# Scores of windowed attention in a different bank layout, v in five slots, and a new instruction list

## The chip, the core and the metric

One NeuronCore of a Trainium2 chip runs the whole program. Time is device time in microseconds (us) of one execution. TensorE (PE in the rows) multiplies; VectorE (DVE), ScalarE (ACT) and GpSimd (POOL) do the elementwise work; SyncE (SP) issues every DMA. Results of TensorE lie in 8 PSUM banks of 128 x 512 fp32.

## What is computed

Two parts, one feeding the other, all in fp32 from the outside:

```python
scores = scale * q @ k.T                     # 8 batches, 8 heads, 576 positions, head_dim 64
rel = pos[:, None] - pos[None, :]
mask = (rel >= 0) & (rel < 128)              # a causal window of 128
scores = where(mask, scores - slope[h] * |rel|, -1e9)
attn = softmax(scores);  x = attn @ v        # heads side by side: x is 576 x 512 per batch
h = gelu_tanh(x @ w_in);  u, g = halves of h
g = layernorm(g) * g_ln
out = x + (u * (w_sg @ g + b_sg)) @ w_out
```

With blocks of 64 positions, a query sees its own key block up to the diagonal, the block before it whole, and of the block before that only the keys that the own block's mask leaves out. So own block and third block share one 64 x 64 square: each place of it belongs to one of the two.

## The kernel before, in words

Heads are taken two at a time: 8 batches x 4 give 32 **pairs**, numbered n = 0 to 31. The gated MLP of a batch b follows its four pairs. All work is cut into **steps**, each a letter and a number, and a list of about 1,900 names (`ORDER`, L803) gives one order from which every engine takes its own steps, in that order. Nothing is reordered behind it: a step that waits holds everything behind it on its engine. `Planner.run` (L408) only gives out the PSUM banks and checks that a buffer is free by then.

Steps of a pair, with the line that runs them: `q` loads q and k (L218, one DMA of 576 KB), `L` loads v (L225 to L229); `a` and `c`, from pair 5 on together as `*`, are the scores on TensorE (L244); `A B C G` are the minima on VectorE, one for each head and two tiles of 128 queries: a `copy_predicated` (L272) folds the third block into the own block's square, and two `tensor_tensor_reduce` (L263, three where the first 64 queries are) add the bias and keep the row's extreme; `e E f F` are the exponentials on ScalarE (L281), `j` those of the first 64 queries; `R` (L293, L294) makes the inverse sums on VectorE; `s S r` scale on GpSimd (L298); `t T z` transpose on TensorE (L308, L321); `X Y` split a transposed bank by a mask (L316, L317) and write `px`; `P` copies the first queries' part (L324); `V` multiplies by v (L340, L345, L349); `x` gathers (L360, L362), `h l k` split into two fp32r parts.

The MLP's steps (`u v tt y O` on TensorE, L576 to L578, L660 to L662, L724, L725) are fp32r products in three terms. The opening also splits the int64-viewed fp64 weights w_in into two parts: `i` load (L167), `d` (L178, L180) on ScalarE, `b o` on VectorE (L182, L184), `+` on GpSimd (L187), `H` and `-`. `w` are single products of the first batch, used as soon as their quarter of the weights is split. `D` (L777) stores the output.

**Scores.** fp32 products have two matmul records each in the trace. A product here has a 64 x 64 stationary part, so the array holds four at a time: head j uses array rows 64j on, and the query half picks the array columns. Before, query half 0 of both heads goes to PSUM partitions 0 to 63 and half 1 to partitions 64 to 127, and each tile of 128 queries fills 192 columns (three key blocks) for either half.

**v.** `vt` has ten slots of 64 + 64 rows, and seven DMAs fill them, with each block of v present twice.

**The masks.** `sel` (128 x 128 uint8) steers the fold, `m_own` the split, `bias` (128 x 256 for each head, L134, ScalarE) the slopes; they are made before the first step.

Of the kernel before, what the change touches and what calls it, by code (L numbers as in the profile page):

```python
# [9 lines left out]
F32 = mybir.dt.float32  # L10
# [11 lines left out]
def attention_gmlp(  # L22
# [19 lines left out]
    P = 128  # L42
# [18 lines left out]
    psum = [ps.tile([P, 512], F32, name=f"bank{i}") for i in range(NB)]  # L61
    given = []
# [23 lines left out]
    ident = const.tile([P, P], F32, name="ident")  # L86
    make_identity(nc, ident)


# [3 lines left out]
    def twice(x):  # L93
        nc.scalar.copy(x[R:P], x[0:R])

    def temp(name, dt=F32):
        return mlp.tile([P, P], dt, name=name, tag="g", bufs=NF)[0:R, 0:R]

    ones = temp("ones")
    nc.vector.memset(ones, 1.0)  # L100


    m_own = halves("m_own", 4 * R)
    lo = temp("lo")
    nc.gpsimd.affine_select(out=lo, in_=ones, pattern=[[1, R]], compare_op=ALU.is_ge, fill=0.0, base=0, channel_multiplier=-1)
    nc.vector.memset(m_own, 1.0)

    for rs, cs in ((slice(R, P), slice(0, 2 * R)), (slice(0, R), slice(2 * R, 4 * R))):
        nc.scalar.copy(m_own[rs, cs].rearrange("p (h c) -> p h c", h=2), over(lo, 2))

    sel_f = temp("sel_f")
    nc.gpsimd.affine_select(out=sel_f, in_=ones, pattern=[[1, R]], compare_op=ALU.is_gt, fill=0.0, base=0, channel_multiplier=-1)
    sel = halves("sel", 2 * R, U8)
    for rs in (slice(0, R), slice(R, P)):
        nc.scalar.copy(sel[rs, 0:R], sel_f)
        nc.scalar.activation(sel[rs, R:2 * R], sel_f, AF.Copy, scale=-1.0, bias=1.0)


# [4 lines left out]
    rel = mlp.tile([P, NF, S], F32, name="rel", tag="u")[:, 0, 0:4 * R]  # L123
    nc.vector.tensor_copy(rel[0:R, 0:R], rel_i)
    nc.vector.tensor_scalar(rel[0:R, R:2 * R], rel[0:R, 0:R], float(R), None, ALU.add)
    nc.vector.scalar_tensor_tensor(out=rel[0:R, 0:R], in0=sel_f, scalar=float(P), in1=rel[0:R, 0:R], op0=ALU.mult, op1=ALU.add)
    nc.scalar.copy(rel[0:R, 2 * R:4 * R].rearrange("p (b c) -> p b c", b=2), over(rel[0:R, 0:R], 2))
    twice(rel)
    nc.vector.scalar_tensor_tensor(out=rel[0:R, 3 * R:4 * R], in0=sel_f, scalar=1e9 / min(slopes), in1=rel[0:R, 0:R], op0=ALU.mult, op1=ALU.add)

    biases = []
    for h in range(H):
# [4 lines left out]
    p0s = [const.tile([P, R], F32, name=f"p0_{i}") for i in range(3)]  # L137

    e0s = []
    for i in range(2):  # L140
        x = const.tile([P, 2 * R], F32, name=f"e0_{i}")
        nc.gpsimd.memset(x, 0.0)
        e0s.append(x)

    NS = 2 * (T + 1)
    stats = []
    for i in range(3):
        x = const.tile([P, 2, NS + 1], F32, name=f"stats{i}")
        nc.vector.memset(x, 1.0)
        stats.append(x)  # L150


# [52 lines left out]
    class Pair:  # L205


        def __init__(self, n):
            self.n, self.b, self.hp = n, n // NPAIR, n % NPAIR
            self.p0 = p0s[n % 3]  # L210
            self.nm, self.sm = [stats[n % 3][:, i, :] for i in range(2)]
# [694 lines left out]
```

## Time and profile before

| what | value |
|---|---|
| time before | 611.9 us, median of 3 runs: 607.64, 611.9, 612.24 |
| the profiled execution | 608.44 us, its span 606.7 us, mean granted clock 0.987 |
| busy: TensorE, VectorE, ScalarE, GpSimd | 580.5, 377.5, 364.9, 231.4 us |
| HBM read, written | 47.88, 9.44 MB |

The span is from the first to the last instruction; 1.7 us lie around it. The profile page gives busy time by engine and by 40 slices, then groups of instructions by source line. Two matmuls overlap in the pipeline, so TensorE's busy time says when it worked and not how fast; how far one start is behind the next tells that.

### The profile page before, as it was taken

The numbers are of one execution on the slowest core, as the hardware profiler recorded it, in microseconds if no ns is written. First come the engines' busy times: TensorE is split into PE (matmuls) and PEld (weight loads), VectorE is DVE, ScalarE is ACT, GpSimd is POOL, SyncE is SP. The second block draws the span as 40 slices with busy tenths as digits, with TensorE's granted clock in tenths as the row PEclk, the third lists the DMA queues.
The fourth block names the chain that finished last, engine by engine and source line by source line (L and its number), as shares of the span: only waits on it lengthen the run. The fifth ranks groups of instructions, "written<-read, shape, count | busy, mean of one in ns | idle before, by whom it ended". The sixth has DMA issues, their size and how long they took to land.

```text
span 606.7 us, 16591 instructions
## 1 busy us (share of the span) xinstructions
PE 580.5 (96%) x6496; PEld 535.9 (88%) x6496; DVE 377.5 (62%) x1348; ACT 364.9 (60%) x1145; POOL 231.4 (38%) x234
## 2 busy tenths in 40 slices
PE   3679999999999999999999999999999999999997
PEld 3457999899898999999999899998999899998997
DVE  5898988566574775456846675746747367625422
ACT  9789796733755459483776549563384656543420
POOL 3677556530173312713164322524118330461030
PEclk8879999999999999999999999999999999999999
DMA  8997533213062425403150175222243013200102
GB/s 259 254 258 206 134 83 87 86 59 88 37 182 72 95 68 139 119 10 98 46 142 2 59 182 127 85 79 88 68 120 98 7 58 107 86 2 1 40 21 97
DMA packets 56450, 58.39 MB, mean 96 GB/s; under 512 B 4914, under 2 KB 45874, under 8 KB 56372
## 3 DMA queue, kind: packets, MB, share of 16 engines
q1 hardware_dynamic: 56372, 57.34, 34.2%
q8 instruction: 51, 0.84, 0.6%
q14 instruction: 27, 0.22, 0.1%
HBM read 47.88 MB, written 9.44 MB: 94 GB/s over the span
## 4 chain that ended last, share of the span: by engine, by line
PE 88%; DMA 6%; SPq 2%; ACT 1%; POOL 1%; issue 1%; DVE 0%; POOLq 0%
PE bank L576 22%; PE bank L577 21%; PE bank L578 21%; PE bank L244 7%; PE bank L340 5%; PE bank L308 4%; PE bank L345 3%; DMA qk<-qkT 3%; PE bank L725 1%; PE bank L724 1%; DMA vt<-v_in 1%; PE bank L660 1%; PE bank L662 1%; SPq L227 1%; DMA wst<-w_in 1%; POOL g L739 1%
## 5 line engine op out<-in xcount | busy, mean ns | idle before, releaser
L281 ACT ACTIVATE e<-e,stats 128x128 f32<-128x128 f32 (+1 forms) x320 | 121.2, 381 | 31.5 <-DVE stats L263 31.0
L298 POOL TENSOR_TENSOR e<-e,rr 128x512 f32<-128x512 f32 (+1 forms) x96 | 79.8, 850 | 151.6 <-DVE rr L294 139.0
L576 PE MATMUL bank<-ws,vn 128*128 128x288 f32 x256 | 78.3, 306 | 0.0
L576 PE MATMUL bank<-g,wo 128*128 128x288 f32 x256 | 77.7, 304 | 0.0
L576 PE MATMUL bank<-xs,wi 128*128 128x288 f32 x256 | 76.8, 300 | 0.0
L577 PE MATMUL bank<-g,wo 128*128 128x288 f32 x256 | 75.7, 296 | 0.3 <-POOL g L739 0.3
L578 PE MATMUL bank<-g,wo 128*128 128x288 f32 x256 | 75.6, 295 | 0.0
L578 PE MATMUL bank<-xs,wi 128*128 128x288 f32 x256 | 75.6, 295 | 0.0
L577 PE MATMUL bank<-xs,wi 128*128 128x288 f32 x256 | 75.6, 295 | 0.0
L577 PE MATMUL bank<-ws,vn 128*128 128x288 f32 x256 | 75.5, 295 | 0.0
L578 PE MATMUL bank<-ws,vn 128*128 128x288 f32 x256 | 75.4, 295 | 0.0
L601 POOL TENSOR_TENSOR rs<-rs,mhalf 128x1 f32<-128x1 f32 (+1 forms) x40 | 29.7, 746 | 112.3 <-DVE rs L598 112.2
L244 PE MATMUL bank<-qk 64*64 64x192 f32 (+2 forms) x1280 | 56.6, 319 | 12.2 <-DMA qk<-qkT 12.2
L263 DVE CUSTOM_DVE_ANT_0 e<-bank,bias 128x128 f32<-128x128 f32 (+1 forms) x256 | 59.2, 269 | 2.3
L739 POOL TENSOR_TENSOR g<-u,g 128x576 fp32r<-128x576 f32 x32 | 45.3, 1431 | 39.8 <-ACT g L736 32.5
L281 ACT ACTIVATION_READ_ACCUMULATOR e<-e,stats 128x1 f32 (+1 forms) x320 | 60.4, 189 | 0.0
L244 PEld LDWEIGHTS bank<-qk 64*64 64x64 f32 x1280 | 45.5, 141 | 15.8 <-DMA qk<-qkT 13.4
L316 DVE TENSOR_TENSOR px<-bank,m_own 128x512 f32<-128x512 f32 x64 | 43.7, 682 | 22.2 <-PE bank L308 17.8
L370 POOL TENSOR_TENSOR xs<-xf,xs 128x576 fp32r<-128x576 f32 x32 | 45.3, 1422 | 29.0 <-ACT xs L367 29.0
L272 DVE COPY_PREDICATED bank<-sel,bank 128x128 f32<-128x128 uint8 x128 | 36.5, 285 | 28.1 <-PE bank L244 28.1
L576 PE MATMUL bank<-wi,xs 128*128 128x512 f32 x128 | 51.8, 404 | 1.6 <-ACT xs L367 1.6
L578 PE MATMUL bank<-wi,xs 128*128 128x512 f32 x128 | 50.9, 397 | 1.8 <-POOL xs L370 1.8
(109 smaller groups left out, 1451.8 us busy)
## 6 DMA issues: line engine op xcount, KB each, us to landing
qk<-qkT SPq DMA_DIRECT2D x32, 576.0 KB, 4.4
vt<-v_in SPq DMA_DIRECT2D x192, 64.0 KB, 3.5
outT<-xf SPq DMA_DIRECT2D x32, 288.0 KB, 2.4
vt<-v_in SPq DMA_DIRECT2D x32, 256.0 KB, 4.5
wst<-w_in SPq DMA_DIRECT2D x8, 512.0 KB, 6.1
wst<-w_out SPq DMA_DIRECT2D x4, 512.0 KB, 4.5
wst<-w_sgT SPq DMA_DIRECT2D x4, 288.0 KB, 5.5
wst<-w_sgT SPq DMA_DIRECT2D x2, 144.0 KB, 4.7
```

Of the source, the lines that this page charges most:

```text
L244: return lambda: nc.tensor.matmul(dst, qk[js, 0, q0:q0 + R], qk[js, 1, k0:k1], start=True, stop=True)
L263: nc.vector.tensor_tensor_reduce(out=dst, in0=src, in1=bs, scale=-1.0 / math.sqrt(D), scalar=3e38, op0=ALU.add, op1=ALU.min, accum_out=acc)
L272: nc.vector.copy_predicated(bank[:, 2 * R:4 * R].rearrange("p (i c) -> p i c", i=2), sel.rearrange("p (i c) -> p i c", i=2), ends)
L281: nc.scalar.activation(x, x, AF.Exp, bias=self.nm[0:n, i:i + 1], scale=-1.0, accum_out=self.sm[0:n, i:i + 1])
L298: nc.gpsimd.tensor_tensor(x, x, self.rr[0:n, i:i + m].rearrange("p (m o) -> p m o", o=1).broadcast_to([n, m, c]), ALU.mult)
L316: nc.vector.tensor_tensor(xv[:, 0], cv, over(m_own, 2), ALU.mult)
L340: return lambda: nc.tensor.matmul(dst(q)[heads[j]], vt[:, PAIR_SLOT[q], heads[j]], px[j][:, (q - 1) * R:q * R], start=(q in (1, 3)), stop= ...
L370: nc.gpsimd.tensor_tensor(lo_of(self.xs), self.xf, hi_of(self.xs).bitcast(F32), ALU.subtract)
L576: nc.tensor.matmul(dst, ah, bh, start=(first and i == 0), stop=False)
L577: nc.tensor.matmul(dst, ah, bl, start=False, stop=False)
L578: nc.tensor.matmul(dst, al, bh, start=False, stop=(last and i == n - 1))
L739: nc.gpsimd.tensor_tensor(st[f"g{f}"][:, 1, :], st["u"][:, f, :], st[f"g{f}"][:, 0, :].bitcast(F32), ALU.subtract)
```

## The change

- **Scores** (L244 before): each query block's own and previous key block are 128 columns at the front of a 256-column half bank, the third key block lies at columns 128 on of it. Of the two query blocks of a tile, one has its three key blocks in one product of 192 columns, the other one of 128 and one of 64. Head 1 swaps the partition halves against head 0. The first 64 queries take the place of the third block that query block 1 doesn't have. 24 products a pair instead of 20, 1,536 streamed columns a head instead of 1,600.
- **Fold**: `copy_predicated` now works on 128 x 2 x 128 instead of 128 x 2 x 64, with a mask `sel0` or `sel1` for either head. The parts of the banks it may read are cleared once at the start (`clear`, eight memsets on VectorE).
- **First queries**: both heads' in columns 64 to 127 of `e0`, head 0 on rows 0 to 63 and head 1 on rows 64 to 127, so one exponential of 128 x 64 in place of two of 64 x 64; after the transpose they lie on rows 64 to 127.
- **v**: five slots, three DMAs (256, 32 and 32 KB) instead of seven (256 and six of 64 KB).
- **Sums**: the 1e-9 is written once beside each sum, and `tensor_reduce` over the two replaces `tensor_scalar`.
- **Gather**: three copies instead of four. **Split**: a mask for each head, same number of elements.
- **Setup**: biases of heads 2 to 7 on GpSimd, `ident` and the split masks later.
- **Output**: in the last batch, each quarter is stored in two DMAs of 144 KB.
- **A new ORDER**, of which two or three places are shown below.

The diff, cut to its core:

```diff
+    def clear(x):
+        nc.vector.memset(x.rearrange("p (t c) -> p t c", t=2)[:, :, P:2 * P], 0.0)
...
+    def bias(h):
         x = halves(f"bias{h}", 4 * R)
-        nc.scalar.activation(x, rel, AF.Copy, scale=-slopes[h] * math.sqrt(D))
+        of = rel[:, h % 2 * 4 * R:(h % 2 + 1) * 4 * R]
+        if h < 2:
+            nc.scalar.activation(x, of, AF.Copy, scale=-slopes[h] * math.sqrt(D))
+        else:
+            nc.gpsimd.tensor_scalar(x, of, -slopes[h] * math.sqrt(D), None, ALU.mult)
...
-            vt = self.vt = att.tile([P, 2 * T + 2, 2 * D], F32, name="vt", bufs=2)
-            blocks = v[b, :, c0:c0 + 2 * D].rearrange("(k p) d -> p k d", p=R)
-            nc.sync.dma_start(vt[0:R, 0:2 * T, :], blocks[:, 0:2 * T, :])
-            for slot, k in ((0, 1), (1, 2), (2, 0), (3, 2)):
-                nc.sync.dma_start(vt[R:P, slot:slot + 5:4, :], blocks[:, k:k + 5:4, :])
-            for rs, k in ((slice(0, R), 4), (slice(R, P), 3)):
-                nc.sync.dma_start(vt[rs, 2 * T:2 * T + 2, :], blocks[:, k:k + 5:4, :])
+            vt = self.vt = att.tile([P, T + 1, 2 * D], F32, name="vt", bufs=2)
+            src = v[b, :, c0:c0 + 2 * D]
+            nc.sync.dma_start(vt[:, 0:T, :], src[0:T * P].rearrange("(k p) d -> p k d", p=P))
+            nc.sync.dma_start(vt[0:R, T, :], src[T * P:S])
+            nc.sync.dma_start(vt[R:P, T, :], src[0:R])
...
             for i in range(2):
-                for half in range(2):
-                    q0 = R + (t2 + i) * P + half * R
-                    for j, js in enumerate(heads):
-                        dst = banks[j][half * R:(half + 1) * R, i * W:(i + 1) * W]
-                        if q0 < P:
-                            insts += [score(dst[:, 0:R], js, q0, 0, R), score(dst[:, R:W], js, q0, 0, P)]
-                        else:
-                            insts.append(score(dst, js, q0, q0 - P, q0 + R))
-            if t2 == 0:
-                insts += [score(banks[j][0:R, 2 * W:2 * W + R], js, 0, 0, R) for j, js in enumerate(heads)]
+                q, d = 1 + 2 * (t2 + i), 4 * i
+                insts += [score(j, 0, d, q, q - 1, q + 1) for j in range(2)]
+                insts += [score(j, 1, d, q + 1, q - 1, q + 2) for j in range(2)]
+                insts += [score(j, 0, d + 3, q, q - 2, q - 1) if q > 1 else score(j, 0, d + 3, 0, 0, 1) for j in range(2)]
...
-            ends = bank.rearrange("p (k c) -> p k c", c=R)[:, 0:6:5, :]
-            nc.vector.copy_predicated(bank[:, 2 * R:4 * R].rearrange("p (i c) -> p i c", i=2), sel.rearrange("p (i c) -> p i c", i=2), ends)
+            sv = bank.rearrange("p (t c) -> p t c", t=2)
+            nc.vector.copy_predicated(sv[:, :, 0:P], sels[j][:, 0:2] if t2 == 0 else sels[j][:, 1:3], sv[:, :, P:2 * P])
...
         def exps_first(self):
-            for j in range(2):
-                self.exp(self.e0[0:R, j * R:(j + 1) * R], 2 * T + j)
+            self.exp(self.e0[:, R:P], 2 * T)
...
-            nc.vector.tensor_scalar(rr, self.sm, 1e-9, None, ALU.add)
+            nc.vector.tensor_reduce(out=rr, in_=self.sm, axis=mybir.AxisListType.X, op=ALU.add)
...
+            insts = [both(t, s, j) for t in range(T) for s in range(2) for j in range(2)]
+            for t in range(T):
+                insts += [rest(t, 0, j) if t else first(j) for j in range(2)]
+                insts += [rest(t, 1, j) for j in range(2)]
             burst(insts)
...
-            add(f"D{b}{c}", "SP", 0.5, at, lambda: nc.sync.dma_start(out[b, cs, :], x[c]), [f"oa{b}{c}0", f"oa{b}{c}1"], lag=2.5)
+            if b == B - 1:
+                for i in range(2):
+                    add(f"D{b}{c}{i}", "SP", 0.5, at, lambda i=i: nc.sync.dma_start(out[b, cs, halves[i]], x[c][:, halves[i]]), [f"oa{b}{c}{i}"], lag=2.5)
```

Rows of the order show the new list at the places below; each row is a source line (of before or of the change), an operation, what it writes from what it reads, and its size. First, TensorE before: the end of V of pair 5 (L345 and L349, px and p times v) and the start of the scores of pair 6 (L244).

```order
L349 MATMUL bank_67<-p_2_126,vt 64x64
L345 MATMUL bank_70<-px,vt 64x64
L349 MATMUL bank_70<-p_2_126,vt 64x64
L244 MATMUL bank_72<-qk 64x64
L244 MATMUL bank_72<-qk 64x128
L244 MATMUL bank_69<-qk 64x64
L244 MATMUL bank_69<-qk 64x128
L244 MATMUL bank_72<-qk 64x192
L244 MATMUL bank_69<-qk 64x192
```

TensorE of the change, the scores (L254) of a whole pair's burst at their end, and the V (L339) that follows them; the MLP's products stand ahead of such a burst and behind such a V.

```order
L254 MATMUL bank_68<-qk 64x128
L254 MATMUL bank_70<-qk 64x128
L254 MATMUL bank_68<-qk 64x192
L254 MATMUL bank_70<-qk 64x192
L254 MATMUL bank_68<-qk 64x64
L254 MATMUL bank_70<-qk 64x64
L339 MATMUL bank_72<-px,vt 64x64 x2
L339 MATMUL bank_71<-px,vt 64x64 x2
```

The scores of a tile of queries went from one product of 192 columns in each of the four array parts to 128, 192 and 64, and a V now follows a burst where a burst followed a V. From pair 5 to the end a burst directly behind a V occurs 21 times before and 6 times in the change, and a V directly behind a burst 3 times and 20 times.

SP before, the DMAs of the opening up to the loads of pairs 4 and 5 (qk x2): two loads of v with seven DMAs each and two of w_in.

```order
L225 DMA vt<-v_in 64x8x128
L227 DMA vt<-v_in 64x2x128 x4
L229 DMA vt<-v_in 64x2x128 x2
L167 DMA wst<-w_in 128x512
L225 DMA vt<-v_in 64x8x128
L227 DMA vt<-v_in 64x2x128 x4
L229 DMA vt<-v_in 64x2x128 x2
L167 DMA wst<-w_in 128x512
L218 DMA qk<-qkT 128x1152 x2
```

SP of the change, the same stretch.

```order
L238 DMA vt<-v_in 128x4x128
L239 DMA vt<-v_in 64x128
L240 DMA vt<-v_in 64x128
L180 DMA wst<-w_in 128x512
L238 DMA vt<-v_in 128x4x128
L239 DMA vt<-v_in 64x128
L240 DMA vt<-v_in 64x128
L180 DMA wst<-w_in 128x512
L566 DMA gb<-g_ln 128x512
L231 DMA qk<-qkT 128x1152 x2
```

Ahead of pair 4's qk, one w_in load of 512 KB fewer and each of the three v loads half as large; a load of 256 KB (gb) moved ahead of it.

ScalarE before, at the start: after the first two biases come six more, then the first copies of a weight (L178, L180).

```order
L94 COPY rel<-rel 64x256
L134 ACTIVATE bias_108<-rel 128x256
L134 ACTIVATE bias_110<-rel 128x256
```

ScalarE of the change, the same place: head 0's bias (bias_109), which the first minimum needs, stands behind the two copies of a weight (L191, L193) that wait for that weight's DMA.

```order
L119 COPY rel<-rel 64x256
L118 COPY rel<-rel 64x256
L191 ACTIVATE wst<-wst 128x512
L127 ACTIVATE bias_113<-rel 128x256
L193 ACTIVATE tmp<-wst 128x512
L127 ACTIVATE bias_109<-rel 128x256
```

The biases of the first two heads went from ahead of the first weight to between and behind its two copies.

## Rows read from the trace of the kernel before

**Rows 1.** The page: span, and busy time by engine.
```profile
span 606.7 us, 16591 instructions
PE 580.5 (96%) x6496; PEld 535.9 (88%) x6496; DVE 377.5 (62%) x1348; ACT 364.9 (60%) x1145; POOL 231.4 (38%) x234
```
**Rows 2.** Stretches: us, busy by engine with counts, granted clock, DMA share, GB/s.
```profile
30.00:45.00 15.00, 10.36 (x171) 8.08 (x171) 14.26 (x54) 13.31 (x46) 12.27 (x11) 0.77 0.92 259
45.00:60.00 15.00, 13.96 (x169) 10.76 (x166) 12.37 (x49) 14.75 (x58) 11.12 (x10) 1.00 0.71 196
300.00:400.00 100.00, 100.00 (x1213) 93.83 (x1206) 62.80 (x252) 67.05 (x210) 41.13 (x39) 1.00 0.35 91
```
**Rows 3.** TensorE's waits, whole span: us in total, times, longest.
```profile
PE bank L244 <- DMA qk<-qkT: 12.2, 5, 4.7
```
**Rows 4.** TensorE's waits from 60 us on.
```profile
PE bank L244 <- DMA qk<-qkT: 2.0, 2, 1.2
```
**Rows 5.** The ending chain in order of time: start us, us, what.
```profile
35.30 5.68 DMA qk<-qkT
41.03 1.00 PE bank L244 x20
...
143.41 0.64 SPq L227
...
147.35 5.77 DMA qk<-qkT
153.16 3.12 PE bank L244 x64
...
603.10 0.46 DVE xf L762
```
**Rows 6.** The chain where a V follows a burst of scores.
```profile
101.19 1.58 PE bank L244 x34
102.77 1.08 PE bank L340 x32
...
104.57 0.48 PE bank L308 x3
```
**Rows 7.** The chain where a burst of scores follows a V.
```profile
173.95 1.08 PE bank L340 x32
...
175.76 1.48 PE bank L244 x31
177.24 0.58 PE bank L308 x4
```
**Rows 8.** Groups by line and shape: line, engine, shapes, count, busy us, mean ns.
```profile
L244 PE MATMUL bank<-qk 64*64 64x192 f32 x896 | 55.8, 348 | 0.0
L244 PE MATMUL bank<-qk 64*64 64x64 f32 x256 | 21.5, 235 | 12.2 <-DMA qk<-qkT 12.2
L345 PE MATMUL bank<-px,vt 64*64 64x64 f32 x896 | 22.3, 227 | 0.0
L272 DVE COPY_PREDICATED bank<-sel,bank 128x128 f32<-128x128 uint8 x128 | 36.5, 285 | 28.1 <-PE bank L244 28.1
L293 DVE TENSOR_SCALAR rr<-stats 128x11 f32<-128x11 f32 x32 | 9.1, 286 | 26.8 <-ACT e L281 26.8
```
**Rows 9.** VectorE's sum operation: shortest, median, longest ns.
```profile
L293 DVE TENSOR_SCALAR rr<-stats x32: 108/172/1261, 14.4 to 531.0; 128x11 f32<-128x11 f32 x32
```
**Rows 10.** VectorE and ScalarE in order of time: start, us, what.
```profile
6.91 0.29 DVE L263 CUSTOM_DVE_ANT_1 e<-bank,bias 128x128 f32<-128x128 f32 x1
...
7.34 0.66 ACT L178 ACTIVATE wst<-wst 128x512 int32<-128x512 uint32 x1
```
**Rows 11.** The stretch from 8.57 to 51.20 us, columns as in Rows 2.
```profile
8.57:51.20 42.63, 27.88 (x442) 21.43 (x443) 38.00 (x155) 37.42 (x143) 32.05 (x28) 0.84 0.93 257
```
**Rows 12.** Loads of v: count, KB each, median us from issue to landing.
```profile
vt<-v_in SPq DMA_DIRECT2D x192, 64.0 KB, 3.5
vt<-v_in SPq DMA_DIRECT2D x32, 256.0 KB, 4.5
```

More of the change, by code (lines that the diff above doesn't have):

```diff
@@ L85, in attention_gmlp @@
     nc.scalar.activation(warm, mhalf, AF.Exp)
-    ident = const.tile([P, P], F32, name="ident")
-    make_identity(nc, ident)
     def halves(name, n, dt=F32):
         return const.tile([P, n], dt, name=name)
-    def twice(x):
-        nc.scalar.copy(x[R:P], x[0:R])
     def temp(name, dt=F32):
-        return mlp.tile([P, P], dt, name=name, tag="g", bufs=NF)[0:R, 0:R]
+        return const.tile([P, R], dt, name=name)[0:R]
     ones = temp("ones")
     nc.vector.memset(ones, 1.0)
[L103 to L111, printed above, removed]
+    for x in psum[0:4]:
+        clear(x)
+    half = [slice(0, R), slice(R, P)]
+    lo, sel_f = temp("lo"), temp("sel_f")
     nc.gpsimd.affine_select(out=sel_f, in_=ones, pattern=[[1, R]], compare_op=ALU.is_gt, fill=0.0, base=0, channel_multiplier=-1)
[L113 to L116, printed above, removed]
     slopes = [2.0 ** (-8.0 * (h + 1) / H) for h in range(H)]
@@ L131, in attention_gmlp @@
+    nc.vector.scalar_tensor_tensor(out=kinds[0:R, 3], in0=sel_f, scalar=1e9 / min(slopes), in1=own, op0=ALU.mult, op1=ALU.add)
+    nc.vector.tensor_copy(kinds[0:R, 2], kinds[0:R, 0])
+    nc.vector.tensor_copy(kinds[0:R, 4:8:2], over(kinds[0:R, 1], 2))
+    nc.vector.tensor_copy(kinds[0:R, 5:8:2], over(kinds[0:R, 0], 2))
+    nc.scalar.copy(rel[R:P, 0:4 * R], rel[0:R, 4 * R:8 * R])
+    nc.scalar.copy(rel[R:P, 4 * R:8 * R], rel[0:R, 0:4 * R])
     biases = []
-    for h in range(H):
+    def bias(h):
@@ L139, in attention_gmlp @@
+        biases.append(x.rearrange("p (b c) -> p b c", b=4))
+    for x in psum[4:]:
+        clear(x)
+    sels = [halves(f"sel{j}", 3 * P, U8).rearrange("p (t c) -> p t c", t=3) for j in range(2)]
+    for x in sels:
+        nc.gpsimd.memset(x, 0)
+    for j, x in enumerate(sels):
+        bias(j)
+        nc.scalar.copy(x[half[j], 1:3, R:P], over(sel_f, 2))
+        nc.scalar.activation(x[half[1 - j], :, 0:R], over(sel_f, 3), AF.Copy, scale=-1.0, bias=1.0)
     e0s = []
     for i in range(2):
-        x = const.tile([P, 2 * R], F32, name=f"e0_{i}")
+        x = const.tile([P, P], F32, name=f"e0_{i}")
@@ L153, in attention_gmlp @@
+    m_owns = [halves(f"m_own{j}", P) for j in range(2)]
+    for j, x in enumerate(m_owns):
+        nc.gpsimd.memset(x, 1.0)
+    for j, x in enumerate(m_owns):
+        nc.scalar.copy(x[R:P, half[j]], lo)
+        nc.scalar.activation(x[0:R, half[1 - j]], lo, AF.Copy, scale=-1.0, bias=1.0)
+    for h in range(2, H):
+        bias(h)
+    p0s = [const.tile([P, P], F32, name=f"p0_{i}") for i in range(3)]
     wi = const.tile([P, 2, NC, 2 * F], F32R, name="wi")
@@ L351, in values, with dst, src @@
-            insts = [pair(q, j) for a, b in ((1, 3), (2, 4), (5, 7), (6, 8)) for q in (a, b) for j in range(2)]
-            insts += [old(3, 0), old(2, 0), old(3, 1), old(2, 1), old(4, 0), old(5, 0), old(4, 1), old(5, 1)]
-            insts += [old(7, 0), old(6, 0), old(7, 1), old(6, 1), old(8, 0), first(1), old(8, 1), first(0)]
+            def dst(t, s, j):
+                return x1[s][heads[j], t * R:(t + 1) * R]
+            def src(rs, i, t, s, j):
+                c0 = (i * T + t) * P
+                return px[j][rs, c0 + (s ^ j) * R:c0 + (s ^ j) * R + R]
```

219 lines of the change are left out of this document (107 added, 112 removed).

## The prediction

> **What bounds the kernel now.** I read the page first, then TensorE's busy time by stretch, then its waits, then the ending chain. The page gives TensorE 580.5 of 606.7 us [rows 1]. In a stretch of the middle it is busy for all of 100 us at full granted clock, with VectorE at 62.80 and ScalarE at 67.05 [rows 2]. There only the length of TensorE's own list counts. In the opening it is otherwise: from 30 to 45 us TensorE works 10.36 us of 15 at a mean granted clock of 0.77, while VectorE works 14.26, ScalarE 13.31, and the DMA engines are 0.92 busy [rows 2]. Three resources are near their limit there at once. TensorE's waits say the same: 12.2 us for qk in all [rows 3], of which 2.0 us fall from 60 us on [rows 4]. So there are four places to cost: the opening, TensorE's list, the later waits, and the end.
>
> **Burst of scores.** The chain shows a pair's burst as 1.48 us where a V is ahead of it [rows 7] and 1.58 us where the MLP or a transpose is ahead and a V behind it [rows 6]. Is it paid by columns or by products? 64x64 records last 235 ns and 64x192 records 348 ns in the trace [rows 8], so 128 columns more take 113 ns and 64 columns some 55. The busiest array part carries 832 columns before (64, 128, 192, 64 for the first tiles, twice 192 for the rest), 13 units of 64, each streamed by two records: 13 x 2 x 0.055 = 1.43 us, close to the 1.48. So columns on the busiest part set it, and the four parts run side by side. The change puts 768 on every part, 12 units: 1.32. That is -0.11 a burst; I take -0.10 for two more weight loads on the part. 27 whole bursts follow the opening: **-2.7 us**. The other end: 40 records in 1.48 us are 37 ns each, and eight more at that price would be +0.30 a burst, +8.1 us. What issue alone allows: 896 64x64 records of V's second part keep TensorE busy for 22.3 us [rows 8], 25 ns each at most, and 48 records in 1.38 us would need 29. So I stay with columns.
>
> **Order of V and burst.** From the start of the V to the transposes behind the burst are 177.24 - 173.95 = 3.29 us [rows 7]. With the burst first and the V behind it: 104.57 - 101.19 = 3.38 us [rows 6]. The second order costs 0.09 us more; it looks like one more change of the array's layout. The new list has it 20 times instead of 3: 17 x 0.09 = **+1.5 us**. Bounds: nothing, and 0.2 each where a product behind also starts late, +3.4.
>
> **Loads.** v goes from 640 KB in seven DMAs to 320 KB in three; medians to landing are 3.5 and 4.5 us for 64 and 256 KB [rows 12]. From 60 us on the waits for qk are two, 2.0 us in all [rows 4]; the chain of the longer one runs from SP's issues of v (0.64 us for one) into a qk DMA of 5.77 us, and the burst at 153.16 waits for that [rows 5]. Four issues less per pair take most of that queue away. I count **-2.0 us**. Bounds: all of it stays (0), or new waits of the same kind come (a rival below).
>
> **The opening.** Two limits, worked out apart. By bytes: what is issued up to pair 4's qk is five qk, eight w_in, three w_sg and three v, 9,760 KB, landed at about 41.0 us [rows 5]; the burst there is what TensorE waits for. In the change it is five qk, seven w_in, three w_sg, three half as large v and gb: 8,544 KB. 1,216 KB fewer at 259 GB/s [rows 2] are 1.25 MB / 259 = 4.8 us earlier. That is the far end, -4.8.
>
> By VectorE: between its first weight step and the px of pair 3 (8.57 to 51.20 us) it is busy 38.00 of 42.63 us and idle 4.63 [rows 11]. In that work stand 20 folds. A fold takes 285 ns [rows 8]; with twice the columns it lies between 285 and 570, I take 418 (half of the price is fixed): 20 x 0.13 = +2.7. Also four sums: the operation has a median of 0.172 us but a longest of 1.261 [rows 9], and a mean of 0.286 [rows 8], so something holds it at times. `tensor_reduce` over 18 numbers should cost about the median. Gain between 1.1 (the longest alone) and 3.6 (all of 32 x 0.114); I take 2.0. And the start: the first minimum runs at 6.91 us, and the first weight's copies at 7.34 [rows 10]. In the change the bias it needs stands behind both copies and the other head's bias. With 0.66 us for a copy [rows 10] and, for want of a row, a fold's 0.3 for a bias, it is there at 7.34 + 1.3 + 0.6 = 9.2 at the latest; if the weight lands right after ScalarE's last setup copy, perhaps at 6, at 7.9. So the first minimum is 1.0 to 2.3 us late; I take 1.5. Sum on VectorE: +2.7 - 2.0 + 1.5 = +2.2 with its idle unchanged, and -2.4 if its 4.63 us of idle vanish. Most of that idle should go: ScalarE, on which VectorE waits, loses six biases and, in five pairs, an exponential with its accumulator read and one gather copy, and the weights land earlier. I take three of the 4.63, **-0.8**, rounded to -1.0 because two weights' steps are also put behind the V of pair 3. The eight clears lie before the first qk has landed, and the biases on GpSimd before its first weight; they are costed at nothing, and if that cover were gone they would be 2.4 and 1.8 us at the same 0.3.
>
> On the sum operation the Trainium skill speaks against the edit: the page VectorE: DVE Perf Modes, section Rules for kernel authors, calls `tensor_reduce` the slowest VectorE operation, always in the plain mode. The trace has no such operation to agree or not; by that rule each sum would be a little longer than the shortest now, some 0.1 us x 32 = 3 us of VectorE as an estimate, in stretches where it is idle a third of the time. What the rule leaves out is the 1.26 us above. The sum stays as it is.
>
> **End.** The last addition starts at 603.10 and lasts 0.46, the span ends at 606.7 [rows 1, 5]: 3.1 us for one store of 288 KB. By the loads of v, 192 KB more take 1.0 us [rows 12], so 144 KB fewer are 0.75; I take **-0.5**, bounds 0 and -0.75.
>
> **Costed at nothing.** Later folds: about 110 x 0.13 = 14 us of VectorE, hidden where it is busy 62.80 of 100 us [rows 2]; if that cover were gone at one place, a pair's transposes would come 0.26 us later per two folds. Fewer exponentials, gather copies and scale elements: off the path after the opening.
>
> **Sum.** -2.7 + 1.5 - 2.0 - 1.0 - 0.5 = -4.7 us. Against the profiled execution of 608.44 that is 603.7; its span of 606.7 becomes 602.0. The median shown is 611.9, 3.5 above the profiled one; from it the sum gives 607.2. As runs of either height are to be expected, I name **606.0**.
>
> **Rivals.**
> *The opening follows the bytes* (-4.8 instead of -1.0): sum -8.5, 599.9 to 603.4. For it: TensorE's wait at 41.03 ends with a DMA [rows 5]. Against it: VectorE is at 14.26 of 15 then [rows 2]. Chance 0.25.
> *The burst is paid by product, not by column*: the small third-block products are started one after the other, and all 24 products pay. +0.30 instead of -0.10 on 27 bursts, +10.8: sum +6.1, slower, 614.5 to 618. The other terms come to -2.0, so it decides from +0.08 us a burst. Against it: 37 ns a record when a 64x192 record streams some 165 ns means four at a time [rows 7, 8]. Chance 0.08.
> The Trainium skill has this as a rule: TensorE: Matmul & The Clock Gate, Part 3: Packing small matmuls, says matmuls start and end strictly in program order. With both records of a product on one array part, two products at most would overlap, and before's burst would take some 20 x 0.165 = 3.3 us; the trace's 1.48 does not agree, so the rule adds nothing to the 0.08.
> *The new list brings waits of its own*: a step ahead of its data by about a microsecond at four or five places, as at 153.16 [rows 5]. +4 to +5: sum about zero, 608 to 612. Nothing in the trace of before can exclude it, as the list is new as a whole; for the list: it leaves, in TensorE time, about as much room between burst and transposes as the old. Chance 0.15.
> *The change does nothing here*: columns are not the burst's limit, VectorE's start eats the opening, only the end gains: -0.5 to -2. Chance 0.12.
>
> **How the numbers follow.** The forecast has 0.40, the rivals 0.25, 0.08, 0.15 and 0.12. The forecast's own range is 602 to 608.5. The range holds the bytes' case but for its lowest edge and the waits' case: 599 to 611; left out are the slow burst and the ends of both, about 0.2. A measurement of this kernel can tell about 1%, 6 us. Faster by over 1%: the bytes' case 0.25 and the lower third of the forecast, 0.14: 0.39. Slower: the slow burst, 0.08, and the worst of new waits, 0.04: 0.12. The rest, 0.49, is within 1%.
>
> **What would show it.** The burst directly behind a V at 1.38 us in the chain: the column count. V and burst together at 3.28: the order. No wait of TensorE for qk after 60 us. Pair 4's qk landed at 36 us, TensorE at pair 4's scores at about 38 to 40, waiting for VectorE and not a DMA. The fold's mean at 0.42 us; the sum's longest under 0.3. Wrong it would be by a burst over 1.6, by waits of several us after 60 us, or by an opening that ends before 37 us.

## The result, and the profile after

The changed kernel takes 601.9 us (median of 4 runs, 601.90 to 601.93) against 610.6 for the kernel before (4 runs, 607.64 to 612.24): a ratio of 0.986, 95% interval 0.982 to 0.991. It is faster by 1.4%, and by 0.9% against the lowest of those four. The prediction named 606.0 in a range of 599 to 611, with 0.39 on faster by over 1%.

The page of the changed kernel, answering to [rows 1]: the span is 6.5 us shorter. VectorE has 23 us more work, ScalarE 25 less.

```profile
span 600.2 us, 16886 instructions
PE 577.7 (96%) x6752; PEld 539.2 (90%) x6752; DVE 400.1 (67%) x1355; ACT 339.5 (57%) x1037; POOL 234.0 (39%) x247
```

Stretches, columns as in [rows 2]. From 30 to 60 us VectorE is now busy 28.4 of 30 us, while the DMA engines' share falls from 0.92 and 0.71 to 0.60 and 0.56.

```profile
30.00:45.00 15.00, 13.06 (x218) 10.41 (x219) 14.20 (x55) 13.71 (x46) 10.80 (x12) 0.67 0.60 198
45.00:60.00 15.00, 13.17 (x158) 10.41 (x157) 14.16 (x52) 14.17 (x50) 12.79 (x11) 1.00 0.56 176
300.00:400.00 100.00, 100.00 (x1273) 94.53 (x1268) 65.82 (x244) 56.28 (x186) 40.40 (x39) 1.00 0.20 63
```

TensorE's waits over the whole span (us in total, times, longest). Of the 12.2 us for qk [rows 3] 1.9 stand under that name. The 4.8 us put down to VectorE's L113 are a wait for qk too: the first scores start at 4.83 us, just after the first qk has landed (4.70), as they did before (4.68 and 4.64). So 6.7 are left. The largest is a new one: pair 0's transposes wait 5.4 us for GpSimd's scaling and start at 17.79 us. Before, they started at 16.48, after waits of 4.0 us for the second qk and 1.8 for GpSimd. The last row is all that falls behind 60 us: the two waits of [rows 4] are gone.

```profile
PE bank L308 <- POOL e L298: 6.8, 3, 5.4
PE bank L254 <- DVE rel L113: 4.8, 1, 4.8
PE bank L254 <- DMA qk<-qkT: 1.9, 1, 1.9
PE bank L254 <- DVE minima L266: 1.8, 1, 1.8
...
PE bank L576 <- POOL g L738: 0.2, 1, 0.2
```

The chain at the place of [rows 6], a burst with its V behind it (start us, us, what). The burst takes 1.49 instead of 1.58. And the V takes 1.71 (102.68 to 104.39) instead of 1.80, which no term of the sum had.

```profile
101.19 1.49 PE bank L254 x35
102.68 1.08 PE bank L339 x32
103.76 0.20 PE bank L347 x2
104.02 0.36 PE bank L344 x26
104.39 0.59 PE bank L308 x4
```

The groups that answer to [rows 8], and the six biases that moved to GpSimd (L129):

```profile
L254 PE MATMUL bank<-qk 64*64 64x192 f32 x512 | 53.2, 350 | 0.0
L254 PE MATMUL bank<-qk 64*64 64x64 f32 x512 | 38.9, 227 | 0.0
L272 DVE COPY_PREDICATED bank<-sel,bank 128x256 f32<-128x256 uint8 x128 | 54.0, 422 | 14.2 <-PE bank L254 13.5
L293 DVE TENSOR_REDUCE rr<-sums 128x9 f32<-128x18 f32 x32 | 5.4, 169 | 28.9 <-ACT e L282 28.8
L129 POOL TENSOR_SCALAR bias<-rel 128x256 f32<-128x256 f32 x6 | 5.1, 863 | 2.9 <-ACT rel L119 2.7
```

For what follows I read each TensorE step from its first record to the first of the next step, from 60 us on (medians, us). "V first" is a V with a burst behind it, "burst first" the other order.

| kernel | V first: V, burst | sum | burst first: burst, V | sum |
|---|---|---|---|---|
| before | 1.713, 1.573 | 3.286 | 1.581, 1.803 | 3.384 |
| changed | 1.597, 1.443 | 3.040 | 1.485, 1.707 | 3.192 |

The last matmul ends at 597.06 instead of 603.06 us, 6.0 earlier, and what lies behind it is 3.14 instead of 3.68.

### The profile page after: what moved, and what is told of

It reads as the page before. It is cut to its first block, busy times and chain, and to the rows that moved or that the text cites. A ratio compares the mean times of both kernels' runs of the same rounds, so it can differ in the third digit from the quotient of the medians.

```text
span 600.2 us, 16886 instructions
## 1 busy us (share of the span) xinstructions
PE 577.7 (96%) x6752; PEld 539.2 (90%) x6752; DVE 400.1 (67%) x1355; ACT 339.5 (57%) x1037; POOL 234.0 (39%) x247
## 4 chain that ended last, share of the span: by engine, by line
PE 91%; DVE 4%; ACT 2%; DMA 1%; POOL 1%; issue 1%; POOLq 0%; SPq 0%; DVEq 0%; ACTq 0%
PE bank L575 22%; PE bank L576 22%; PE bank L577 22%; PE bank L254 7%; PE bank L339 6%; PE bank L308 4%; PE bank L344 2%; PE bank L724 1%; DVE e L266 1%; PE bank L723 1%; PE bank L659 1%; PE bank L347 1%; PE bank L661 1%; DMA wst<-w_in 1%; DVE bank L272 1%
## 5 line engine op out<-in xcount | busy, mean ns | idle before, releaser
L282 ACT ACTIVATE e<-e,minima 128x128 f32<-128x128 f32 (+1 forms) x288 | 110.7, 388 | 27.9 <-DVE minima L266 27.5
L298 POOL TENSOR_TENSOR e<-e,rr 128x512 f32<-128x512 f32 (+1 forms) x96 | 75.7, 810 | 121.6 <-DVE rr L294 118.8
L266 DVE CUSTOM_DVE_ANT_0 e<-bank,bias 128x128 f32<-128x128 f32 (+1 forms) x320 | 76.0, 275 | 9.6 <-ACT bias L127 1.6
L254 PE MATMUL bank<-qk 64*64 64x128 f32 (+2 forms) x1536 | 54.9, 290 | 9.2 <-DVE rel L113 4.8
L272 DVE COPY_PREDICATED bank<-sel,bank 128x256 f32<-128x256 uint8 x128 | 54.0, 422 | 14.2 <-PE bank L254 13.5
L254 PEld LDWEIGHTS bank<-qk 64*64 64x64 f32 x1536 | 50.1, 142 | 14.7 <-DVE rel L112 4.8
L282 ACT ACTIVATION_READ_ACCUMULATOR e<-e,minima 128x1 f32 x288 | 54.8, 190 | 0.0
L575 PE MATMUL bank<-wi,xs 128*128 128x512 f32 x128 | 51.8, 405 | 0.1
L730 DVE TENSOR_TENSOR u<-bank,u 128x288 f32<-128x288 f32 x64 | 27.4, 449 | 36.4 <-PE bank L724 34.6
```

The lines of the kernel that those rows point to most:

```text
L254: return lambda: nc.tensor.matmul(banks[j][half[s ^ j], dst * R:(dst + k1 - k0) * R], qk[heads[j], 0, q * R:(q + 1) * R], qk[heads[j], 1, ...
L266: nc.vector.tensor_tensor_reduce(out=dst, in0=src, in1=bs, scale=-1.0 / math.sqrt(D), scalar=3e38, op0=ALU.add, op1=ALU.min, accum_out=acc)
L272: nc.vector.copy_predicated(sv[:, :, 0:P], sels[j][:, 0:2] if t2 == 0 else sels[j][:, 1:3], sv[:, :, P:2 * P])
L282: nc.scalar.activation(x, x, AF.Exp, bias=self.nm[0:n, i:i + 1], scale=-1.0, accum_out=self.sm[0:n, i, 0:1])
L298: nc.gpsimd.tensor_tensor(x, x, self.rr[0:n, i:i + m].rearrange("p (m o) -> p m o", o=1).broadcast_to([n, m, c]), ALU.mult)
L575: nc.tensor.matmul(dst, ah, bh, start=(first and i == 0), stop=False)
```

## The experiments

All times are medians. Each kernel ran beside the kernel before on the same chip, which took 608.2 to 610.8 in the four groups. The changed kernel itself ran with the result alone, so a difference to its 601.9 compares two groups, and one of about 1 us is trusted here only where the traces show it.

**The code and the list, each alone.** First the changed code with the list of before (the lists stand in words here):

```diff
-        ORDER = (the changed list)
+        ORDER = (the list of before, D7c written as D7c0 D7c1)
```

> The changed code with the list of the kernel before (only the last batch's stores named as two). Theory, the gain is in the code: bursts -2.6, V -2.9, qk waits -2.0, end -0.5, and the +1.5 of the new order of V and burst not paid: about -8 against before, ratio 0.987. A burst with V behind it 1.48 instead of 1.58, a V with the MLP behind it 1.70 instead of 1.80. Rival, the new list is what brings the gain (it spares TensorE waits that the old one has): ratio 0.995 to 1.000, with waits of TensorE for VectorE and ScalarE after 60 us.

Measured: 601.15, ratio 0.985 (0.981 to 0.988). Theory held: the code alone brings all of the gain, and the new list nothing that can be told (601.15 against 601.9). Behind 60 us TensorE waits 0.3 us in all, so the two waits for qk go with the code, by either list. On this one list the two codes can be laid side by side, step by step, from the first step of batch 0's MLP (61.17 us before, 61.58 here) to the last matmul: 7.8 us less, of which V makes 3.1, 26 bursts 3.2 and the two waits for qk 2.4 as read from step to step, while small new waits take 0.9 back. Then the code of before with the changed list:

```diff
-        ORDER = (the list of before)
+        ORDER = (the changed list, D7c0 D7c1 written as D7c)
```

> The code of before with the changed list (the last batch's stores unsplit). Theory: only the order of V and burst changes, 17 x 0.09 = +1.5 us, and the waits for qk of before, 2.0 us after 60 us, stay: ratio 1.00 to 1.005; bursts 1.58 and V 1.80 with the MLP behind them. Rival, the list is the gain: ratio 0.990 to 0.995.

Measured: 615.8, ratio 1.008 (1.006 to 1.011). The rival falls; the list alone costs some 5 us by the ratio, more than the 0 to 3 of the theory. Its waits over the whole span:

```profile
PE bank L244 <- DMA qk<-qkT: 12.6, 4, 4.7
PE bank L308 <- POOL e L298: 6.4, 3, 3.7
PE bank L321 <- POOL e L298: 2.0, 2, 1.7
```

With the old, larger loads the waits for qk are there again, 1.8 us of them in one behind 60 us. The order of V and burst is 1.6 us of the 5 by the table above (16 x 0.098). How the rest is split I did not settle.

**V's small products.** V's second part is made of 64x64 products, each on one of four parts of the array (rows 0-63 or 64-127, by output half). Before, the parts carry 5, 4, 4 and 3 of them, because the first queries of the even heads stand on rows 0-63. In the changed kernel all first queries are on rows 64-127 and each part carries 4. Two kernels change this. In the first, the changed kernel has the even heads' first queries on rows 0-63 again:

```diff
-    nc.tensor.matmul(dst(T, 0, j), vt[half[1], T, heads[j]], self.p0[half[1], half[j]], ...
+    nc.tensor.matmul(dst(T, 1 - j, j), vt[half[j], T, heads[j]], self.p0[half[j], half[j]], ...
```

The first queries' part is copied whole for it, and gathered by one copy more, both on ScalarE.

> The changed kernel with the first queries of the even heads put back on rows 64 to 127's neighbour, the array part of rows 0 to 63, so that the four array parts carry 5, 4, 3 and 4 small products of V instead of 4 each. Leaves out: the even heads' first 64 queries get weights of zero. Theory, the busiest part ends V: V with the MLP behind it 1.70 -> 1.80, +0.10 x 32 = +3.2 us on the changed kernel, ratio to before 0.991 to 0.992. Rival, the 24 products are paid by number or by the transfer of v: V stays at 1.70, ratio as the changed kernel's, 0.986. The bursts stay at 1.485 by both.

In the second, the kernel before has them on rows 64-127, and the gather reads them where they land; nothing else changes:

```diff
-    nc.tensor.matmul(x1[1 - j][heads[j], ...], vt[heads[j], 2 * j, heads[j]], self.p0[heads[j]], ...
+    nc.tensor.matmul(x1[0][heads[j], ...], vt[heads[1], 2, heads[j]], self.p0[heads[1]], ...
```

> The kernel before with one edit: the first queries of the even heads go through the array part of rows 64 to 127 as the odd heads' do, so that the parts carry 4 small products of V each instead of 5, 4, 4, 3. Leaves out: the even heads' first 64 queries are weighted by the odd heads' numbers. Theory: V with the MLP behind it 1.80 -> 1.70, -0.10 x 32 = -3 us, ratio 0.995. Rival, V's gain in the changed kernel came with v's five slots or the new layout of its columns: V stays 1.80, ratio 1.000.

Measured: the first 605.1, 3.2 more than the changed kernel (ratio to before 0.990, 0.987 to 0.994), as the theory had it; in its trace the 28 V's after the opening make 2.7 us of this, and one V that waits 0.65 us (at 81.8 us) most of the rest. The second 609.0, ratio 0.998 (0.995 to 1.001): by time alone this can't be told from no change. Its trace tells it. The chain at the same V, first of the kernel before with only this edit, then of the changed kernel with it undone:

```profile
101.63 1.08 PE bank L340 x32
102.71 0.55 PE bank L345 x25
...
103.34 0.59 PE bank L308 x4
```

```profile
103.56 1.08 PE bank L339 x32
104.65 0.20 PE bank L347 x2
...
104.91 0.46 PE bank L344 x25
105.37 0.59 PE bank L308 x4
```

The large products take 1.08 in both. The small ones take 0.63 us with four on each part (102.71 to 103.34) and 0.72 with five on one (104.65 to 105.37). With a transpose behind it, V is 1.707 us in the edited kernel before and 1.804 in the edited changed one, against 1.804 and 1.708 without the edits. The cause is shown both ways: the busiest part ends V. The last matmul of the edited kernel before is 3.3 us earlier than that of before: 0.9 are there at the MLP's first step, V gives 3.1 behind it, and longer waits, those for qk above all, take 0.8 back. Its profiled execution is also the lowest of its times (605.2 to 614.0 us), so the price of V is read from the single V, 0.10 us, and not from these sums.

**Columns or products.** The 192-column products of the scores cut in two, columns unchanged:

```diff
-    insts += [score(j, 1, d, q + 1, q - 1, q + 2) for j in range(2)]
+    insts += [score(j, 1, d, q + 1, q - 1, q + 1) for j in range(2)]
+    insts += [score(j, 1, d + 2, q + 1, q + 1, q + 2) for j in range(2)]
```

> The changed kernel with each 192-column product of the scores cut into one of 128 and one of 64 columns: 32 products (64 records) in a whole burst instead of 24 (48), the same 768 columns on every array part. Theory, the burst is paid by columns of the busiest part: burst behind a V 1.485 -> 1.49 to 1.58 (two more weight loads on half of the parts), 0 to +2.7 us in all. Rival, by product: 1.485 / 48 = 31 ns a record, so 1.98 a burst, +0.5 x 27 = +13 us, ratio to before 1.007.

Measured: 602.24, 0.3 more than the changed kernel, where the rival asked for 13. A burst with a V behind it goes from 1.485 to 1.498 us with 64 records instead of 48. So the burst is not paid by the number of its products. What a further product costs on the busiest part this run can't show: the split takes two parts from four products to eight, and the other two had eight already. That columns on the busiest part set the burst fits the table above: from before to the changed kernel the columns of all parts together fell by 4.0%, those of the busiest part by 7.7%, and the burst by 6.1% (V behind) and 8.3% (V ahead). No run changes the busiest part's columns alone.

**The loads of v.** Four DMAs of 64 KB more per pair, into a tile that nothing reads:

```diff
+    again = att.tile([P, 4, 2 * D], F32, name="again", bufs=1)
+    blocks = src.rearrange("(k p) d -> p k d", p=R)
+    for rs in half:
+        for c in range(2):
+            nc.sync.dma_start(again[rs, 2 * c:2 * c + 2, :], blocks[:, c:c + 5:4, :])
```

> The changed kernel with four more DMAs of 64 KB for each pair's v, into a tile that nothing reads: seven DMAs and 576 KB as against three and 320 KB (before: seven and 640 KB). Theory, the loads of v made the waits for qk after 60 us: one or two such waits come back, 1 to 2 us, and in the opening pair 4's qk lands some 3 us later (four pairs' 1 MB at 259 GB/s is 4 us), which TensorE sees only in part: +1 to +4 us on the changed kernel, ratio to before 0.988 to 0.993. Rival, the list alone removed those waits (it puts the qk loads earlier): no wait for qk after 60 us, ratio 0.986.

Measured: 606.1, ratio 0.995 (0.993 to 0.997): 4.2 us more than the changed kernel, the top end of the theory. To see how much an edit costs the opening, I read when TensorE begins u000, one of the first two u steps of batch 0's MLP, in kernels that share a list. Here 2.6 of the 4.2 us are there by then (64.17 to 66.73 us), and a wait for qk is back behind 60 us:

```profile
PE bank L259 <- DMA qk<-qkT: 1.0, 1, 1.0
```

The times scatter again too: they spread over 2.4 us here, over 4.4 to 7.3 for the kernel before in the four groups, and over 5.3 and 8.8 for the two other kernels with the old loads. With the small loads alone no kernel spreads over more than 1.2, and the changed kernel over 0.03. So the scatter goes with the loads of v, though these four DMAs bring only a part of it back, and how they make it was not looked into.

**The biases.** Those of the first two heads on GpSimd, the other six on ScalarE, in the changed kernel and then in the changed code with the old list:

```diff
-        if h < 2:
+        if h >= 2:
             nc.scalar.activation(x, of, AF.Copy, scale=-slopes[h] * math.sqrt(D))
```

> The changed kernel with the biases the other way round: those of the first two heads on GpSimd, which is idle then, the other six on ScalarE. Theory, two thirds of the late start of the opening come from them (the first minimum waits 1.6 us for a bias that stands behind the first weight's copy on ScalarE; GpSimd's first weight step waits 2 us for six biases of 0.86 us): first minimum 8.56 -> 7.0 us, GpSimd's first weight step 11.90 -> 10.0, transposes of pair 0 at 17.79 -> 16.3, and what of it lasts to the end 0.5 to 1.5 us: ratio to before 0.984 to 0.985. Rival, the opening is bound later, by VectorE's and ScalarE's work from 15 to 50 us: same time as the changed kernel, ratio 0.986, the start of the MLP (first step of the first batch behind V of pair 3) where it was, at 64.2.

> The changed code with the list of the kernel before, and the biases swapped between GpSimd and ScalarE. Theory: this list has the order V, burst nearly everywhere, and the late start costs it as much as it costs the changed kernel: 601.15 - 1.0 = 600.1. Rival, its opening is bound by the loads (its second burst waits for qk until 10.9 us): no gain, 601.1.

Measured: 600.87, ratio 0.986 (0.982 to 0.989), and 598.74, ratio 0.981 (0.978 to 0.983). The first is 1.0 less than the changed kernel, the second 2.4 less than with the old list alone. The intervals overlap in both cases; the traces tell. GpSimd in order of time, in the changed kernel, then in the one with the biases swapped (start, us, what, idle before):

```profile
5.96 5.32 POOL L129 TENSOR_SCALAR bias<-rel 128x256 f32<-128x256 f32 x6 [2.68 <-ACT rel L119]
11.90 1.29 POOL L200 TENSOR_TENSOR tmp<-tmp,wst 128x512 int32<-128x512 int32 x1 [0.62 <-issue]
```

```profile
5.96 1.79 POOL L129 TENSOR_SCALAR bias<-rel 128x256 f32<-128x256 f32 x2 [2.68 <-ACT rel L119]
10.91 1.30 POOL L200 TENSOR_TENSOR tmp<-tmp,wst 128x512 int32<-128x512 int32 x1 [3.16 <-ACT e L282]
```

The first weight step on GpSimd moves from 11.90 to 10.91, and VectorE's first minimum from 8.56 to 7.78, both by less than expected. Most of it reaches the end: on the new list u000 comes at 63.42 instead of 64.17, and behind it the two traces agree step by step; on the old list it comes at 59.17 instead of 61.58. On the old list I had expected 1.0 and got 2.4. There the idle time before pair 0's transposes falls from 5.1 to 2.5 us. The first minimum makes little of it (7.77 us instead of 8.07). Two weight operations of VectorE make most of it, here first without the swap and then with it (start, us, what):

```profile
11.92 1.23 DVE L195 TENSOR_SCALAR tmp<-tmp 128x512 int32<-128x512 int32 x1
13.18 1.77 DVE L197 SCALAR_TENSOR_TENSOR tmp<-wst,tmp 128x512 int32<-128x512 int32 x1
```

```profile
11.58 0.42 DVE L195 TENSOR_SCALAR tmp<-tmp 128x512 int32<-128x512 int32 x1
12.03 0.69 DVE L197 SCALAR_TENSOR_TENSOR tmp<-wst,tmp 128x512 int32<-128x512 int32 x1
```

Without the swap GpSimd's six biases put its next two operations at 11.57 to 14.40 us, and VectorE's two, begun while those ran, take 3.0 us instead of 1.1.

The changed code with the old list and swapped biases is the fastest kernel of the study, 3.2 us under the changed kernel. Its page:

```profile
span 597.1 us, 16874 instructions
PE 575.5 (96%) x6752; PEld 538.1 (90%) x6752; DVE 399.2 (67%) x1355; ACT 353.2 (59%) x1049; POOL 231.3 (39%) x243
```

**The sum of the softmax**, by `tensor_scalar` again:

```diff
-    nc.vector.tensor_reduce(out=rr, in_=self.sm, axis=mybir.AxisListType.X, op=ALU.add)
+    nc.vector.tensor_scalar(rr, self.sm[:, :, 0], 1e-9, None, ALU.add)
```

> The changed kernel with its sum of the softmax by tensor_scalar over every second number, as before, instead of tensor_reduce. Theory: the operation takes 0.17 us undisturbed and up to 1.2 us while GpSimd works, mean about 0.29; the opening gets up to 2 us of VectorE back, of which TensorE sees little: 0 to +1 us on the changed kernel, ratio 0.986 to 0.988. Rival, tensor_reduce is itself the slower: ratio 0.985 or less, and a mean at or under 0.17 us for the sum.

Measured: 603.3, 1.4 more than the changed kernel. VectorE's operation at L293 here, then in the changed kernel (shortest, median, longest ns):

```profile
L293 DVE TENSOR_SCALAR rr<-sums x32: 159/173/1286, 15.7 to 525.3; 128x9 f32<-128x9 f32 x32
```

```profile
L293 DVE TENSOR_REDUCE rr<-sums x32: 159/173/175, 15.9 to 524.5; 128x9 f32<-128x18 f32 x32
```

Equal when undisturbed; of the two only `tensor_scalar` is ever held. The longest stands here with GpSimd's operation beside it (start, us, what): the sum begins while GpSimd's runs and ends at 54.40, 0.03 us after that one ends (54.37).

```profile
53.12 1.29 DVE L293 TENSOR_SCALAR rr<-sums 128x9 f32<-128x9 f32 x1
```

```profile
52.68 1.69 POOL L200 TENSOR_TENSOR tmp<-tmp,wst 128x512 int32<-128x512 int32 x1 [2.71 <-DVE tmp L197]
```

All eight sums over 0.25 us in this trace end like that, 0.02 to 0.04 us behind a GpSimd operation that was running when they began. So the "something" that the prediction saw holding the sum is a running GpSimd operation. The edit's gain is 5.1 us of VectorE (10.5 to 5.4). In the profiled executions 0.8 of it reach the end: u000 comes at 64.17 instead of 64.96, and behind it the two traces agree step by step. Half of the other kernel's runs lie about 1 us higher (603.7 to 603.9, the rest 602.7 to 602.9), which makes its median 1.4; no trace shows why.

**The fold.** A second fold of two columns behind every fold, which writes what stands there already:

```diff
     nc.vector.copy_predicated(sv[:, :, 0:P], ...)
+    nc.vector.copy_predicated(sv[:, :, 0:2], ...)
```

> The changed kernel with a second fold of two columns behind every fold, which writes what stands there already: some 0.15 us more of VectorE a fold (422 ns for 256 columns and 285 for 128 leave 148 for none), about what the change added to each (0.137), twenty of them before the px of pair 3. Theory, the longer fold took back the opening's gain from the smaller loads, as VectorE is busy 14 of 15 us there: the same again, +2.5 to +3 us at the first MLP step (64.2 -> 67) and in the total, ratio to before 0.990 to 0.991, nothing after 60 us. Rival, most of it is hidden behind TensorE and ScalarE: +0 to +0.8 us.

Measured: 607.7, ratio 0.998 (0.996 to 1.000), 5.8 us more than the changed kernel, where the theory had 2.5 to 3.

```profile
L273 DVE COPY_PREDICATED bank<-sel,bank 128x4 f32<-128x4 uint8 x128 | 21.4, 167 | 4.4
```

At 0.167 us a fold u000 comes 3.4 us later (64.17 to 67.53): there the theory holds, twenty folds are 3.3. But a further 2.4 us are lost behind it, at six V's, bursts and groups of transposes, which take 0.1 to 0.8 us longer each, with new waits of TensorE for VectorE and for what it feeds. "Nothing after 60 us" was wrong.

**V ahead of the burst.** Eleven of the changed list's pairs of steps turned round, where pair m's px was done before the burst began; then the same with the biases swapped:

```diff
-        *19 V16 L18 ...
+        V16 *19 L18 ...
```

> The changed kernel with eleven of its twenty pairs of steps 'burst n, V m' turned round to 'V m, burst n', where the px of pair m was done before the burst began. Theory, the order costs 0.15 us a pair in the changed kernel (burst 1.485 and V 1.707 as against V 1.597 and burst 1.443): 11 x 0.152 = -1.7 us on the changed kernel, 600.2, ratio to before 0.982 to 0.984. Rival, the burst comes 1.6 us later for its pair, VectorE and ScalarE get its scores later and TensorE waits at the transposes: same or more time than the changed kernel, with waits over 0.2 us from 185 us on.

> Both at once: the eleven pairs of steps turned round, and the first two biases on GpSimd with the other six on ScalarE (-1.0 us when done alone). Theory: the two add up, as the one acts after 185 us and the other before 15: 600.87 - 1.7 = 599.2, the fastest of all; span 597.8, last matmul 594.6. Rival, as at the turned pairs alone: 600.9 or more.

Measured: 603.95 and 602.96, each 2.1 us more than the same kernel unturned. The theory falls for the sum, though not for the pair: the turned V takes 1.597 and its burst 1.443, the expected 0.15 less, 1.7 us in all. New waits of TensorE take 3.7 us, all of them behind 185 us. These two rows are 2.6 of it; the other 1.1 lie inside two groups of transposes (nine take 1.76 us instead of 0.96, five 0.76 instead of 0.46):

```profile
PE bank L575 <- DVE minima L266: 2.2, 4, 0.6
PE bank L339 <- DVE px L317: 0.4, 1, 0.4
```

One of them in the chain. The MLP step right behind the burst waits for VectorE to read the scores out of the banks:

```profile
423.05 0.74 PE bank L254 x17
...
423.85 0.44 DVE bank L272
...
424.95 0.02 DVE minima L266
424.97 0.04 issue
425.01 0.50 PE bank L575
```

In the changed list the V stands there and covers those 1.7 us. So the order "burst, V" is dearer by 0.15 and buys time for the minima; by this list the cover is worth more than its price.

## Why the prediction came out as it did

The sum was -4.7 us; the profiled span fell by 6.5. By terms:

| term | predicted | measured | from |
|---|---|---|---|
| bursts | -2.7 | -3.2 | 26 bursts, at the old order |
| V | nothing | -3.1 | 28 V's, at the old order |
| order of V and burst | +1.5 | +2.4 | 16 x (3.192 - 3.040) |
| qk waits behind 60 us | -2.0 | -2.0 | [rows 4], none left there |
| opening | -1.0 | about 0 | what is left of -6.0 |
| end | -0.5 | -0.5 | 3.68 to 3.14 |

**Missing: the V.** This is the step that failed. The prediction asked for the busiest array part of a burst (832 columns to 768) and did not ask the same of V, though the change moves the first queries to other rows. The same count gives it: 5, 4, 4, 3 products to 4 each, one product of two records less on the busiest part. That is -0.10 with the MLP behind and -0.12 with a burst behind, and it is worth as much as the bursts.

**Right, a little small: the burst.** -0.096 with a V behind it and -0.130 with a V ahead, for -0.10. Its named sign, 1.38 us behind a V in the chain, is 1.33 there (142.88 to 144.22 us), against the 1.48 of [rows 7]; from first record to first record the two are 1.443 and 1.573. The rival that pays by product is gone: 16 records more cost 0.013 us. With it goes, as before, the rule of strict program order that the prediction named from the Trainium skill (TensorE: Matmul & The Clock Gate, Part 3: Packing small matmuls). This case's traces do not agree with it: 48 records take 1.44 us, 30 ns each, and in the kernel with five products on one part a last record of V starts at 143.94 us, behind three records (143.89 to 143.93) of the burst that follows V in the list.

**Too small: the order.** Predicted from one pair of each kind, 0.09. In the changed kernel the two orders differ by 0.152, since burst and V each gained more in the order that the list left. The named 3.28 for burst and V together is 3.192.

**Right: the waits for qk and the end.** No wait for qk behind 60 us; and the list had no part in it (the old list with the new code has none, and the seven loads bring one back).

**The opening: terms named, balance wrong.** On the same old list u000 begins at 61.17 us before and at 61.58 with the changed code: +0.4 instead of -1.0. These are one execution each, and the old code's opening varies by more: in the edited kernel before u000 begins at 60.25. Its parts, each by its own run on the new list: the smaller loads gave 2.6; the sum gave 0.8 (64.96 to 64.17), for 2.0; the fold cost 3.4 x 0.137/0.167 = 2.8, for 2.7; the biases cost what swapping them gives back, 0.8 on the new list and 2.4 on the old. If they add up, that is +0.2 to +1.8. Two were mis-sized. The biases on GpSimd were "costed at nothing", 1.8 us if uncovered, at 0.3 each by the nearest row, which was VectorE's; they take 0.863 each, 5.3 us in a row, and on the old list what stands behind them on GpSimd also holds VectorE. And the sum's price on VectorE did not come through in full. The late first minimum was right: 1.65 us for 1.5, at 8.56 instead of 6.91 [rows 10]. Pair 4's qk, issued with pair 5's from 28.84 us on with 6.8 us to landing at most, was there by about 36 as named; its scores began at 40.5, not 38 to 40, with no wait for a DMA.

**The rivals.** The opening did not follow the bytes alone: in the changed kernel VectorE is busy 14.20 of 15 us from 30 to 45, with the DMA engines at 0.60. But bytes counted in part, as four more DMAs for each pair's v cost it 2.6 us. The list's own waits did not come in the changed kernel; they came with the code of before, some 5 us dearer by this list, and when I turned its pairs. That the change does nothing is ruled out by the bursts and by V.

**On the sum,** the Trainium skill (VectorE: DVE Perf Modes, Rules for kernel authors) calls `tensor_reduce` the slowest operation of VectorE. On 18 numbers in each partition the trace does not agree: a median of 173 ns for both, and a longest of 175 against 1286.

The point forecast was 4.1 us too high. The terms make 1.7 of that: V by -3.1 and the bursts by -0.5, against +0.9 of the order and +1.0 of the opening. That the sum came within 1.8 us is in part luck, as these errors go against each other. The other 2.3 are the choice of 606.0, above the 603.7 that the sum gave from the profiled execution: it allowed for runs of either height, but the scatter of the kernel before went with the change (0.03 us over four runs).

## What to carry to other kernels

Where small matmuls run side by side on parts of the array, count records and columns on each part, for every stage that a change of layout touches, not only for the one that it names: the busiest part set the time of V here, and the time of the burst fits it. Cost an operation that moves to another engine by that engine's rows, or take its unknown price as a term with two ends; "hidden" for a setup step means to name what stands behind it in that engine's queue. An order of two long steps that looks dearer may be cover for another engine's reading of the banks, so turn it only with the reader's time in hand.

## What the hardware showed that I had not expected

- A 128x256 `tensor_scalar` took 0.863 us on GpSimd and 0.40 us as an activation on ScalarE in the same kernel.
- A short `tensor_scalar` on VectorE, begun while GpSimd ran an operation over 512 or 576 numbers a partition, was mostly held until that one ended, up to 1.29 us; two that began in the last 0.04 us of one were not, and `tensor_reduce` at the same places in the list was not (longest 0.175). Longer operations were held too: a 128x512 `tensor_scalar` of 0.42 us took 1.23, a `scalar_tensor_tensor` of 0.69 took 1.77.
- Cutting eight products in two at equal columns, on the two parts that had the fewer products, cost 0.013 us a burst, while the order of two layouts cost 0.15.
- The clock fell behind a gap of the opening in one kernel and not in the other. TensorE was busy 0.21 us from 14 to 18 us in the changed kernel, and then worked at 0.50, the 1.2 GHz level (first two rows). With the biases swapped it was busy 0.81 us there, and the granted clock stayed at 1.00, the 2.4 GHz level (last two). Columns as in [rows 2].

```profile
14.00:18.00 4.00, 0.21 (x1) 0.22 (x2) 3.59 (x19) 2.25 (x7) 3.09 (x4) 0.74 0.98 320
18.00:22.00 4.00, 4.00 (x49) 3.60 (x52) 3.90 (x14) 3.64 (x17) 2.62 (x3) 0.50 0.54 167
```

```profile
14.00:18.00 4.00, 0.81 (x4) 0.82 (x5) 3.55 (x22) 2.70 (x10) 3.52 (x4) 1.00 0.94 310
18.00:22.00 4.00, 4.00 (x55) 3.53 (x53) 3.86 (x11) 3.88 (x19) 2.68 (x3) 1.00 0.47 162
```
